# A decode step of cached attention and an MLP on one core: order of the K sums, the pieces of the last K tiles, and the gathers of the output weights

## The chip, the cores and the metric

The kernel runs on one core of a Trainium2 chip. The metric is the device time in microseconds (us) of one execution. Five engines work side by side: TensorE (PE, with its weight loads shown as PEld), VectorE (DVE), ScalarE (ACT), GpSimd (POOL) and SyncE (SP), which here only issues DMAs. The transfers themselves are carried out by 16 DMA engines.

## What is computed

Two tokens (a batch of 2, one position each) pass through a layer norm, an attention over a cache of 8192 positions with 32 heads of width 128, the output projection, a residual, and a pre-norm MLP with another residual. All arrays are float32.

```python
def _A_ref(x, k_cache, v_cache, wq, wo):             # x (2,1,512), caches (2,32,8192,128)
    q = (x @ wq).reshape(B, Sq, H, Dh).transpose(0, 2, 1, 3)
    scores = jnp.einsum("bhqd,bhkd->bhqk", q, k_cache) * (Dh ** -0.5)
    p = _softmax(scores, axis=-1)
    o = jnp.einsum("bhqk,bhkd->bhqd", p, v_cache)
    return o.transpose(0, 2, 1, 3).reshape(B, Sq, H * Dh) @ wo      # wo (4096, 512)

def _B_ref(x, w1, b1, w2, b2):
    y = _layernorm(x)
    return _gelu(y @ w1 + b1) @ w2 + b2              # w1 (512,1792), w2 (1792,512)

h = x + _A_ref(_layernorm(x), k_cache, v_cache, wq, wo)
h2 = h + _B_ref(_layernorm(h), w1, b1, w2, b2)
```

## The kernel before

**Tiles.** The caches are read once, in 32 steps of the main loop (`for i in range(NI)`, line 360). Step i takes one of the two tokens (i modulo 2) and one pair of heads (i divided by 2). Its K tile is 8 MB: 128 partitions, 64 for each of the two heads, each with 128 positions of 128 numbers (64 KB). Its V tile has the same shape. K and V tiles share a ring of three buffers (`BUFS = 3`), so a load waits until the tile three places before it in the ring has been used up. The order of loads is v of step i, then k of step i + 1; near the end k of step 31 comes ahead of v of step 30, and v of step 31 is followed by the weights of the MLP, which take the next buffer of the ring. All of these are issued by SP on one queue. `load` (line 65) takes a list of pieces along the positions; `parts_of` (line 355) says into how many pieces the K tiles 29, 30 and 31 are cut (2, 4 and 2), and V of step 31 comes in four pieces of 64, 32, 24 and 8 positions.

**Scores.** For one query row a matrix product would use little of TensorE, so the scores are made on VectorE. A K tile is worked in four chunks c of 32 positions. `multiply` (line 236) multiplies a chunk by the query; `halve` (line 240) has POOL add the upper half of the 128 products to the lower half; `sums` (line 246) adds up what is left on VectorE. For the first three chunks POOL halves all 32 positions, for the last one 12 of them (`NPOOL`); the other 20 are summed at full width. So in step i and chunk c VectorE is given: the product of chunk c, the sum of the halved part of chunk c - 1, and the sum of the part of chunk c that was not halved. Here they are in the program without a rule for their order; a scheduler places them:

```python
            halve(i, c)
            if i > 0 and c == 0 and not late:
                gather(done)
            if c > 0:
                sums(i, c - 1, True)
            sums(i, c, False)
```

**Softmax and V.** `row_max` (line 250) takes the maximum of each partition on VectorE and transposes the result on TensorE (line 253); `all_max` (line 257) takes the maximum over partitions; a small product (line 260) brings it back to all partitions. `exps` (lines 266 and 271) makes the exponentials on ScalarE. `values` (line 294) multiplies them by the V tile on TensorE in 32 blocks; the profile counts two passes for each. All this is done for step i - 1 while the scores of step i are made. `behind(m)` gives instructions a place in the order of issue after the instruction m.

**The last step.** V of step 30 is multiplied inside step 31, as far as block `MOST` = 24, ahead of the transposed maximum of step 31 (lines 422 to 424). The remaining blocks are put behind that step's `all_max` (line 450). Behind them come the blocks of V of step 31 (lines 506 and 512), and then the projection, the layer norm and the MLP (lines 520 to 573), with a few products in between that only keep TensorE busy (line 478).

**The output weights.** The 4096 rows of `wo` are used as heads are finished. The last 256 rows belong to the last pair of heads and have a load of their own (line 384). The other 3840 rows come in groups (`PLAN`, line 29). An entry 4 is a group of 512 rows, 4 rows of 2 KB for each of 128 partitions, loaded by SP. A tuple is a group in which blocks of four partitions, named by their first partition, get no rows; it has 4 rows for each of the others and is loaded by an indirect DMA that POOL issues (line 135), after POOL has cleared the tile (line 134). The indices of that DMA are built once on VectorE (lines 109 to 117): from the first partition of a left-out block on they are raised by 4096, beyond the bound, which leaves these out, and behind the block they are lowered again, by four more than that. There is one buffer for these groups. A group is used when the heads of its last row are finished: `head_out` (line 329) writes the head rows in the group's layout, `turn` (line 337) transposes them, `turned` (lines 344 and 346) adds their product to `rowacc`. In the step after that the next group is loaded (line 386).

The order of instructions on each engine is fixed when the program is built; each engine works through its own list.

Of the kernel before, what the change touches and what calls it, by code (L numbers as in the profile page):

```python
# [21 lines left out]
BUFS = 3  # L22
NG = 4
WARM = 4
MOST = 24
WR = 4


PLAN = [4, 4,
        (4, 12, 20, 24, 36), 4,  # L30
        (4, 36, 68, 72, 76), 4,
        (4, 36, 112, 116, 120, 124), 4]
FAR = 4096


# [1 line left out]
def tile_decode_block(ctx: ExitStack, tc: tile.TileContext, x, k, v, wq, wo, w1, b1, w2, b2, out):  # L37
# [11 lines left out]
    NI = NM * B  # L49
# [15 lines left out]
    def load(src, i, parts):  # L65
        m, b = divmod(i, B)
        t = kv.tile([P, NS, DH], F32, name="kv", tag="kv")
        rows = src[b, QG * m:QG * m + QG].rearrange("h (p j) d -> (h p) j d", j=NS)
        for s0, n in parts:
            nc.sync.dma_start(t[:, s0:s0 + n], rows[:, s0:s0 + n])  # L70
        return t
# [35 lines left out]
    for _, _, _, blocks in groups:  # L107
        if blocks and blocks not in index:
            acc = work.tile([P, 1], F32, name="ixf")
            nc.vector.tensor_copy(acc, part)  # L110
            for s0 in blocks:
                for edge, step in ((s0, FAR), (s0 + 4, -FAR - 4)):
                    one = work.tile([P, 1], F32, name="ix1")
                    nc.vector.tensor_scalar(one, part, edge - 0.5, float(step), op0=ALU.is_ge, op1=ALU.mult)
                    nc.vector.tensor_add(acc, acc, one)
            index[blocks] = const.tile([P, 1], I32, name=f"ix{len(index)}")
            nc.vector.tensor_copy(index[blocks], acc)
# [7 lines left out]
    def load_wo(g, gate=None):  # L125
        r0, n, r, shut = groups[g]
        t = wts.tile([P, WR, D], F32, name="wog")
        wo_g[g] = t
        if not shut:
            nc.sync.dma_start(t[:, :r], wo[r0:r0 + n, :].rearrange("(p r) n -> p r n", r=r))  # L130
            return
        if gate is not None:
            next_of_pool(lambda: nc.gpsimd.tensor_copy(gate0, gate))
        next_of_pool(lambda: nc.gpsimd.memset(t, 0.0))
        next_of_pool(lambda: nc.gpsimd.indirect_dma_start(
            t.rearrange("p r n -> p (r n)"), None, wo_runs, bass.IndirectOffsetOnAxis(index[shut], 0),
            element_offset=r0 * D, bounds_check=n // r - 1, oob_is_err=False))
# [93 lines left out]
    def multiply(i, c):  # L231
        if c == 0:
            ST[i] = work.tile([P, NS], F32, name="s", bufs=3)
        qb = qps[i // B][:, i % B, None, :].to_broadcast([P, CH, DH])
        kc = kt[i][:, c * CH:(c + 1) * CH, :]
        return nc.vector.tensor_tensor(kc, kc, qb, op=ALU.mult)  # L236
# [5 lines left out]
    def sums(i, c, halved):  # L242
        edge = (c + 1) * CH - NPOOL[c]
        a, e, d = (edge, (c + 1) * CH, DH // 2) if halved else (c * CH, edge, DH)
        if a < e:
            nc.vector.tensor_reduce(ST[i][:, a:e], kt[i][:, a:e, :d], axis=AX.X, op=ALU.add)  # L246
# [8 lines left out]
    def all_max(i):  # L255
        gm = work.tile([1, QG], F32, name="gm")
        last = nc.vector.tensor_reduce(gm, MT.pop(i).rearrange("o (e p) -> o e p", e=QG), axis=AX.X, op=ALU.max,  # L257
                                       negate=True)
        GM[i] = psm.tile([P, QG], F32, name="sm")
        nc.tensor.matmul(GM[i], ones[:1, :], gm, start=True, stop=True)  # L260
        return last

    def exps(i):
        m, b = divmod(i, B)
        nb = work.tile([P, QG], F32, name="nb")
        nc.scalar.activation(nb, GM.pop(i), AF.Copy, scale=SCALE)  # L266
        LT[m] = lt2[:, m % 2]
        s = ST.pop(i).rearrange("p (u j) -> p u j", j=4)
        for e in range(QG):
            ps = slice(e * HP, (e + 1) * HP)  # L270
            nc.scalar.activation(ptz[i % 2][ps, :, 4 * e:4 * e + 4], s[ps], AF.Exp, bias=nb[ps, e:e + 1], scale=SCALE,  # L271
                                 accum_out=LT[m][ps, 32 * e + b:32 * e + b + 1])
# [10 lines left out]
    def inverse(i):  # L283
        if i in RL:
            rl = work.tile(list(RL[i].shape), F32, name="rl" if i >= NI - B else "rlr")
            last = nc.vector.reciprocal(rl, RL[i])
            RL[i] = rl
            return last

    def values(i, us=range(NS // 4)):  # L290
        so = so2[i % 2]
        for u in us:
            n = u % NG
            m = nc.tensor.matmul(so[32 * n:32 * n + 4 * QG], ptz[i % 2][:, u, :], vt[i][:, 4 * u:4 * u + 4, :],  # L294
                                 start=(u < NG), stop=(u >= NS // 4 - NG))
        return m
# [44 lines left out]
    def turned(g):  # L341
        n = groups[g][2]
        t = work.tile([P, WR, B], F32, name="ot4")
        nc.vector.tensor_copy(t[:, :n], TP.pop(g)[:, :n])  # L344
        for r in range(n):
            nc.tensor.matmul(rowacc, t[:, r, :], wo_g[g][:, r, :], start=False,  # L346
                             stop=(g == len(groups) - 1 and r == n - 1))

    def behind(m):
        return tc.issue_after(m.ins)  # L350

    def cut(n):
        return [(j * NS // n, NS // n) for j in range(n)]

    parts_of = {NI - 3: cut(2), NI - 2: cut(4), NI - 1: cut(2)}
    kt, vt = {}, {}
    next_load = 0
    free_from = 1
# [1 line left out]
    for i in range(NI):  # L360
        m, b = divmod(i, B)
        done = i - 1
        late = i == NI - 1
        if not late:
            if i < NI - 2:
                vt[i] = load(v, i, cut(1))
        else:
            vt[i] = load(v, i, [(0, 64), (64, 32), (96, 24), (120, 8)])
            b1r = rows2[:, 0].rearrange("p r q -> p (r q)")[:, :FN]
            nc.vector.memset(b1r, 0.0)  # L370
            b2s = rows2[:B, 1].rearrange("b r q -> b (r q)")
            for e in range(B):
                nc.sync.dma_start(b1r[WB * e::32], b1.rearrange("(n f) -> n f", n=NG))
            nc.sync.dma_start(b2s, b2[None, :].to_broadcast([B, D]))
        if i > 0:
            last = all_max(done)
            exps(done)
            if not late:
                values(done)
        if i < NI - 1:  # L380
            kt[i + 1] = load(k, i + 1, parts_of.get(i + 1, cut(1)))
        if i == NI - 2:
            vt[i] = load(v, i, cut(1))
            nc.sync.dma_start(wl, wo[HL * DH:, :].rearrange("(h p) n -> p h n", p=P))
        if next_load < len(groups) and i == free_from:
            load_wo(next_load, MX[i - 1][:1, 0:1] if next_load == 0 else None)
            next_load += 1
            free_from = NI
        for c in range(NC):
            if i > 0 and c == 0:  # L390
                with behind(last):
                    mul = multiply(i, c)
            else:
                mul = multiply(i, c)
            ended = [g for g in group_end.get(done // B, ())] if done >= 0 and done % B == B - 1 else []
            with behind(mul):
                if i > 0 and c == 1:
                    inverse(done)
                if i > 0 and c == 2 and done % B == B - 1:
                    for h in range(done // B * QG, done // B * QG + QG):  # L400
                        head_out(h)
                if c == 3:
                    for g in ended:
                        turned(g)
                        free_from = i + 1
            halve(i, c)
            if i > 0 and c == 0 and not late:
                gather(done)
            if c > 0:
                sums(i, c - 1, True)  # L410
            sums(i, c, False)
            if i > 0 and c == 0:
                total(done)
            if i > 0 and c == 1 and not late:
                head_sum(done)
            if c == 2:
                for g in ended:
                    turn(g)
        sums(i, NC - 1, True)
        if b == B - 1 and m % 2 == 1 and m + 1 < NM:  # L420
            make_q(m + 1)
        if late:
            with behind(values(done, range(MOST))):
                row_max(i)
        else:
            row_max(i)
# [22 lines left out]
    with behind(last):  # L449
        last = values(hl - 1, range(MOST, NS // 4))  # L450
    gather(hl - 1)
# [148 lines left out]
```

## Time and profile before

| | us |
|---|---|
| median of 3 runs | 1309.41 |
| lowest and highest | 1308.73, 1310.24 |
| the profiled execution, whole | 1309.04 |
| its span, first to last instruction | 1307.3 |

| engine | busy us | share of the span |
|---|---|---|
| VectorE | 941.0 | 72% |
| POOL | 501.7 | 38% |
| TensorE, products | 431.9 | 33% |
| TensorE, weight loads | 128.3 | 10% |
| ScalarE | 63.9 | 5% |

The DMAs move 561.48 MB, on average 430 GB/s over the span. The granted clock of TensorE is 0.652 of full speed on average.

In the lists below, a line of the timeline gives the start and the busy time in us, the engine, the line of the program, the operation, the tile written and the tiles read, the shapes, the number of instructions merged, and in brackets the idle time before it with what ended it. A line of the chain of waits gives the start, the length and what the time was spent on; the chain is followed back from the last instruction. A line of the table by stretches gives the stretch, its length, the busy time and the number of instructions for PE, PEld, DVE, ACT and POOL, then the granted clock of TensorE, the busy share of the DMA engines, and GB/s.

### The profile page before, as it was taken

The numbers are of one execution on the slowest core, as the hardware profiler recorded it, in microseconds if no ns is written. First come the engines' busy times: TensorE is split into PE (matmuls) and PEld (weight loads), VectorE is DVE, ScalarE is ACT, GpSimd is POOL, SyncE is SP. The second block draws the span as 40 slices with busy tenths as digits, with TensorE's granted clock in tenths as the row PEclk, the third lists the DMA queues.
The fourth block names the chain that finished last, engine by engine and source line by source line (L and its number), as shares of the span: only waits on it lengthen the run. The fifth ranks groups of instructions, "written<-read, shape, count | busy, mean of one in ns | idle before, by whom it ended". The sixth has DMA issues, their size and how long they took to land.

```text
span 1307.3 us, 7121 instructions
## 1 busy us (share of the span) xinstructions
PE 431.9 (33%) x2893; PEld 128.3 (10%) x2893; DVE 941.0 (72%) x539; ACT 63.9 (5%) x203; POOL 501.7 (38%) x146
## 2 busy tenths in 40 slices
PE   3033214232331334412344303343213434212528
PEld 0001001010110101100011000101001011000103
DVE  3666688766688676688667697676687767698892
ACT  0000000000000000000000000000000000000001
POOL 0433244432354433344333344333344422444440
PEclk9566656766566666756667556666556666556679
DMA  9999999999999999999999999999999999999997
GB/s 417 429 436 434 431 445 422 442 425 442 429 436 430 438 427 438 428 438 433 434 436 436 432 433 433 434 438 429 440 427 438 433 430 436 423 435 429 441 421 305
DMA packets 12869, 561.48 MB, mean 430 GB/s; under 512 B 1488, under 2 KB 1504, under 8 KB 2148
## 3 DMA queue, kind: packets, MB, share of 16 engines
q1 hardware_dynamic: 12400, 558.39, 98.8%
q0 software_dynamic: 432, 2.62, 0.5%
q8 instruction: 23, 0.38, 0.1%
q14 instruction: 10, 0.08, 0.0%
q10 hardware_dynamic: 4, 0.00, 0.0%
HBM read 561.53 MB, written 0.00 MB: 430 GB/s over the span
## 4 chain that ended last, share of the span: by engine, by line
DMA 37%; DVE 24%; issue 16%; PE 14%; POOL 7%; ACT 1%; POOLq 0%; SPq 0%; DVEq 0%
DMA kv<-in_A_k_cache_dram 37%; DVE kv L236 14%; PE so L294 11%; DVE s L246 9%; POOL kv L240 7%; PE rowacc L346 1%; ACT pt L271 1%; DVE orow L329 1%; PE sm L260 1%; PE sm L253 0%; DVE gm L257 0%; DVE mx L250 0%; PE po L569 0%; PE so L543 0%; ACT nb L266 0%
## 5 line engine op out<-in xcount | busy, mean ns | idle before, releaser
L240 POOL TENSOR_TENSOR kv<-kv 128x2048 f32<-128x2048 f32 (+1 forms) x128 | 490.4, 3844 | 754.1 <-DVE kv L236 540.8
L236 DVE TENSOR_TENSOR kv<-kv,qps 128x4096 f32<-128x4096 f32 x128 | 562.4, 4415 | 301.7 <-DMA kv<-in_A_k_cache_dram 301.5
L246 DVE TENSOR_REDUCE s<-kv 128x32 f32<-128x2048 f32 (+2 forms) x160 | 333.9, 2120 | 21.4 <-POOL kv L240 21.1
L294 PE MATMUL so<-kv,pt 128*8 128x512 f32 x2048 | 282.2, 709 | 55.1 <-ACT pt L271 36.0
L253 PE MATMUL sm<-ident,mx 128*1 128x128 f32 x32 | 11.1, 346 | 495.0 <-DVE mx L250 495.0
L294 PEld LDWEIGHTS so<-kv,pt 128*8 128x8 f32 x2048 | 56.4, 100 | 250.3 <-issue 195.3
L346 PE MATMUL rowacc<-wog,ot 128*2 128x512 f32 x64 | 47.4, 910 | 51.8 <-DVE ot L344 32.3
L221 PE MATMUL qps<-q,pick 2*64 2x256 f32 x64 | 13.8, 577 | 128.8 <-DVE kv L236 128.8
L253 PEld LDWEIGHTS sm<-ident,mx 128*1 128x1 f32 x32 | 2.5, 79 | 519.3 <-issue 283.4
L266 ACT ACTIVATE nb<-sm 128x2 f32<-128x2 f32 x32 | 5.5, 172 | 919.5 <-PE sm L260 919.5
L337 PE MATMUL sm<-ident,orow 2*128 2x2 f32 x32 | 4.6, 244 | 104.3 <-DVE orow L329 104.3
L300 ACT ACTIVATE ss<-so 128x512 f32<-128x512 f32 x31 | 18.5, 597 | 269.4 <-PE so L294 269.4
L314 PE MATMUL sm<-ss,selr 128*34 128x128 f32 x240 | 29.8, 278 | 0.7 <-ACT ss L300 0.7
L314 PEld LDWEIGHTS sm<-ss,selr 128*34 128x34 f32 x240 | 25.6, 115 | 1.8 <-ACT ss L300 1.7
L271 ACT ACTIVATE pt<-s,nb 64x128 f32<-64x128 f32 x64 | 25.5, 399 | 1.4
L260 PE MATMUL sm<-gm,ones 1*128 1x2 f32 x64 | 17.0, 333 | 11.5 <-DVE gm L257 11.5
L257 DVE TENSOR_REDUCE gm<-sm 1x2 f32<-1x128 f32 x32 | 8.9, 279 | 16.4 <-PE sm L253 16.4
L221 PEld LDWEIGHTS qps<-q,pick 2*64 2x64 f32 x64 | 5.5, 192 | 138.1 <-DVE kv L236 134.4
L260 PEld LDWEIGHTS sm<-gm,ones 1*128 1x128 f32 x64 | 14.2, 275 | 21.9 <-DVE gm L257 20.2
L346 PEld LDWEIGHTS rowacc<-wog,ot 128*2 128x2 f32 x64 | 6.6, 111 | 84.8 <-issue 52.1
L337 PEld LDWEIGHTS sm<-ident,orow 2*128 2x128 f32 x32 | 4.0, 209 | 106.4 <-DVE orow L329 63.5
L329 DVE TENSOR_SCALAR orow<-sm,rlr 2x128 f32<-2x128 f32 (+6 forms) x43 | 14.0, 355 | 0.2
(104 smaller groups left out, 115.9 us busy)
## 6 DMA issues: line engine op xcount, KB each, us to landing
kv<-in_A_k_cache_dram SPq DMA_DIRECT2D x4, 4096.0 KB
kv<-in_A_k_cache_dram SPq DMA_DIRECT2D x4, 2048.0 KB, 30.7
ws<-in_B_w_dram SPq DMA_DIRECT2D x3, 1792.0 KB, 16.7
wog<-in_A_wo_dram SPq DMA_DIRECT2D x5, 1024.0 KB, 38.1
kv<-in_A_v_cache_dram SPq DMA_DIRECT2D x1, 4096.0 KB, 30.5
kv<-in_A_v_cache_dram SPq DMA_DIRECT2D x1, 2048.0 KB, 34.9
kv<-in_A_v_cache_dram SPq DMA_DIRECT2D x1, 1536.0 KB, 38.1
ws<-in_B_w_dram SPq DMA_DIRECT2D x1, 1024.0 KB, 16.5
```

The source lines that it names most:

```text
L221: nc.tensor.matmul(t[e * HP:(e + 1) * HP, :, b], pick[32 * n:32 * n + B, b, :], rows[:, :, e], start=True, stop=True)
L236: return nc.vector.tensor_tensor(kc, kc, qb, op=ALU.mult)
L240: return nc.gpsimd.tensor_tensor(t[:, :, :DH // 2], t[:, :, :DH // 2], t[:, :, DH // 2:], op=ALU.add)
L246: nc.vector.tensor_reduce(ST[i][:, a:e], kt[i][:, a:e, :d], axis=AX.X, op=ALU.add)
L253: nc.tensor.transpose(MT[i], mx, ident)
L260: nc.tensor.matmul(GM[i], ones[:1, :], gm, start=True, stop=True)
L271: nc.scalar.activation(ptz[i % 2][ps, :, 4 * e:4 * e + 4], s[ps], AF.Exp, bias=nb[ps, e:e + 1], scale=SCALE, accum_out=LT[m][ps, 32 * e + ...
L294: m = nc.tensor.matmul(so[32 * n:32 * n + 4 * QG], ptz[i % 2][:, u, :], vt[i][:, 4 * u:4 * u + 4, :], start=(u < NG), stop=(u >= NS // 4 - ...
L300: return nc.scalar.activation(SS[i], so2[i % 2], AF.Copy)
L314: nc.tensor.matmul(OP[m], sel_row[:, j, B - 1 - c:B - 1 - c + QR], SS[i - 1 + c][:, j * DH:(j + 1) * DH], start=(c == 0 and j == 0), stop= ...
L329: nc.vector.tensor_scalar(orow[g % 2][:B, :r, p0:p0 + run].rearrange("b r p -> b p r"), OP[h // QG][r0e:r0e + B, c0:c0 + run * r].rearrang ...
L346: nc.tensor.matmul(rowacc, t[:, r, :], wo_g[g][:, r, :], start=False, stop=(g == len(groups) - 1 and r == n - 1))
```

## The change

Five things differ.

1. The sums of a step and chunk are given a place in the order of issue behind the product of the same chunk.
2. K tile 29 is loaded in one piece instead of two, tile 30 in two instead of four; tile 31 stays at two.
3. The 3840 rows come in nine groups instead of eight: four with left-out blocks instead of three (384 rows each instead of 432, 432 and 416), four of 512 rows instead of five, and one of 256 rows. The left-out blocks are 32 instead of 16, and other ones. The last group is now one with left-out blocks; it is loaded in step 29 and used in step 30.
4. Where two left-out blocks touch, the table of indices is built without the edge between them.
5. `MOST` is 8 instead of 24.

```diff
-MOST = 24
+MOST = 8

 PLAN = [4, 4,
-        (4, 12, 20, 24, 36), 4,
-        (4, 36, 68, 72, 76), 4,
-        (4, 36, 112, 116, 120, 124), 4]
+        (0, 4, 68, 72, 76, 80, 84, 88), 4,
+        (36, 48, 100, 104, 108, 112, 116, 120), 4,
+        (4, 12, 20, 24, 68, 72, 76, 80), 2,
+        (12, 20, 24, 44, 52, 56, 116, 120)]
...
             nc.vector.tensor_copy(acc, part)
-            for s0 in blocks:
-                for edge, step in ((s0, FAR), (s0 + 4, -FAR - 4)):
+            ends = [p for s0 in blocks for p in (s0, s0 + 4)]
+            for p in sorted(set(ends)):
+                if ends.count(p) == 1:
+                    if p in blocks:
+                        edge, step, first = p, FAR, p
+                    else:
+                        edge, step = p, first - p - FAR
                     one = work.tile([P, 1], F32, name="ix1")
                     nc.vector.tensor_scalar(one, part, edge - 0.5, float(step), op0=ALU.is_ge, op1=ALU.mult)
                     nc.vector.tensor_add(acc, acc, one)
...
-    parts_of = {NI - 3: cut(2), NI - 2: cut(4), NI - 1: cut(2)}
+    parts_of = {NI - 2: cut(2), NI - 1: cut(2)}
...
-            if c > 0:
-                sums(i, c - 1, True)
-            sums(i, c, False)
+            with behind(mul):
+                if c > 0:
+                    sums(i, c - 1, True)
+                sums(i, c, False)
```

## The prediction

> **What bounds the kernel now.** I read the utilisation page first, then the records of the DMA packets, then the chain of waits and the timelines of VectorE and TensorE over the last 130 us.
>
> ```profile
> PE 431.9 (33%) x2893; PEld 128.3 (10%) x2893; DVE 941.0 (72%) x539; ACT 63.9 (5%) x203; POOL 501.7 (38%) x146
> DMA  9999999999999999999999999999999999999997
> q1 hardware_dynamic: 12400, 558.39, 98.8%
> ```
>
> The DMA row is at nine tenths in every slice but the last and the loads' queue alone fills 98.8% of the 16 engines' span, while VectorE has 28% to spare. The packet records say more. A packet starts 3 to 4 ns before another ends, so the records can be strung into 16 streams. None is idle between the first packet and 1293.8 us (but for two gaps of 0.2 us in one), and a 64 KB packet takes 2.418 us in every stream. So up to there only bytes count, and they stay the same (561 MB). What can change is which stream is last, and what the engines do behind the last K tiles:
>
> ```profile
> 1175.42 8.75 DVE L236 TENSOR_TENSOR kv<-kv,qps 128x4096 f32<-128x4096 f32 x2 [1.13 <-DMA kv<-in_A_k_cache_dram]
> 1189.15 2.29 DVE L246 TENSOR_REDUCE s<-kv 128x32 f32<-128x2048 f32 x1 [2.18 <-POOL kv L240]
> ...
> 1209.35 4.42 DVE L236 TENSOR_TENSOR kv<-kv,qps 128x4096 f32<-128x4096 f32 x1 [1.93 <-DMA kv<-in_A_k_cache_dram]
> 1218.59 2.29 DVE L246 TENSOR_REDUCE s<-kv 128x32 f32<-128x2048 f32 x1 [4.82 <-POOL kv L240]
> ...
> 1243.89 8.73 DVE L236 TENSOR_TENSOR kv<-kv,qps 128x4096 f32<-128x4096 f32 x2
> ...
> 1257.44 2.29 DVE L246 TENSOR_REDUCE s<-kv 128x32 f32<-128x2048 f32 x1 [2.17 <-POOL kv L240]
> 1259.65 8.74 DVE L236 TENSOR_TENSOR kv<-kv,qps 128x4096 f32<-128x4096 f32 x2
> 1268.74 5.87 DVE L246 TENSOR_REDUCE s<-kv 128x32 f32<-128x2048 f32 x3 [0.35 <-POOL kv L240]
> 1274.65 0.29 DVE L250 TENSOR_REDUCE mx<-s 128x1 f32<-128x128 f32 x1
> ```
>
> Tile 30 starts at 1209.35 when its first quarter lands (1208.90). From there VectorE is the bound: it waits 4.82 and 2.17 us for GpSimd's halving, and is never again short of K. Behind it TensorE sets the end:
>
> ```profile
> 1275.08 0.37 PE sm L253
> 1275.45 1.81 PE so L294 x2
> 1277.26 0.51 PE sm L260 x2
> 1277.77 2.48 PE so L294 x14
> 1280.26 0.31 PE sm L278 x2
> 1280.57 3.55 PE so L294 x32
> ```
>
> This chain runs on without a gap to the output product at 1300.64; the last packet of w2 landed at 1300.04, and its four products come last in 3.3 us. So the final landing has about 3 us to spare; K's landings and TensorE's queue behind the transpose at 1275.08 (call it T) do not.
>
> **Part 1: order and pieces of the last K tiles.** In the built program only tiles 29, 30 and 31 change order; all others already alternate product, sum, product, sum. Their price is two undisturbed tiles of this trace: tile 27, from its first product (1105.24) to the end of its L257 maximum, 29.2 us; tile 26, the same with a clearing of the bias row, two head rows and a copy, 30.4 us (1066.57 to 1096.95).
>
> When do they start? Tile 29 is now one load. Before, its halves landed at 1175.04 and 1184.72, the latter in the latest stream. By then the changed kernel has moved 3456 rows of wo instead of 3840, and the late streams have rows left out (part 2). Stream by stream I get 1182.4 for the latest. With the 0.5 us from landing to product seen at 1208.90 and 1209.35, tile 29 starts at 1182.9 instead of 1175.4 and ends at 1212.1. VectorE stands idle for these 7 us, which by itself costs nothing: the first half of tile 30 lands at 1212.5 (before 1213.77 for the same bytes), so tile 30 starts at 1213.0. It is tile 26 with four head rows (0.225, 0.41, 0.41, 0.225) instead of two (0.86): 30.8 us, to 1243.8. Its second half (1222.2) is there before its third product. Tile 31, landed at 1241.6, starts at 1243.7; T follows 28.5 us after its first product, as in tile 27: 1272.2. **T comes 2.9 us earlier.** If that cover were gone, each us by which the first half of tile 30 is late would go straight into T.
>
> What hangs on the later end of tile 29: SP may issue the load of tile 31 only when tile 29's buffer is free, now about 1211 instead of 1206. The queue then still holds tile 30 until 1220.3 on the quickest stream, so it costs nothing unless tile 29 ends 8 us later still. The load of v29 waits for tile 28 (1173.3); the quickest stream is dry at 1179.5, before 1177.2. The SP loads queued behind these have more room.
>
> **Part 2: the gathers.** A partition left out shows as a 4 B packet of 9 ns instead of an 8 KB one of 309. In the three gathers, rows 4 and 36 always vanish from the same stream, so I take p and p+32 to share one. A stream moves 64 - 4c packets of 8 KB for wo now and 68 - 4c after, with c its blocks left out; packets follow each other at 0.305 us.
>
> ```
> rows of the stream             c now  after   us      last packet ends now -> after
> 12|20|24, 68|72|76             1      3      -1.2     1297.8..1300.03 -> 1296.6..1298.8
> 112|116|120                    1      3      -1.2     1299.4..1300.00 -> 1298.2..1298.8
> 4 (and 36)                     6      3      +4.9     1293.8 -> 1298.7
> 124                            1      0      +2.4     1296.0 -> 1298.4
> five never left out            0      0 or 1  +1.2 or 0   1296.6..1298.1 -> 1296.6..1299.3
> ```
>
> The spread of 6 us becomes about 2, the end 1.2 us earlier (at worst 0.7): for K this is in the landings above, for w2 it is worth nothing. The fourth gather adds 20 ns of empty packets per stream. On POOL it adds a clearing (1.80) and an issue (1.16) between tiles 28 and 29, where POOL idles for 10.7 us (until 1180.07). The clearing waits for the products of the group before, with tile 29's halving queued behind it; that needs tile 29's first product, now at 1187. It lands 27 us after issue, near 1200, and is used at 1236. The shorter table of edges is built under the first loads (first K tile at 42.6 us).
>
> **Part 3: MOST 24 to 8.** Not in the title, and it costs. v30 lands at 1262.17; TensorE then does 24 of its 32 blocks in 6.72 us, done at 1269.3, long before T. Now 8 go there and 24 come behind T, in front of the last V tile. From T the rows above give 0.30 to the first block, 1.81 for it, 0.51 for L260, 2.5 for eight blocks (now seven), 0.31 for L278: T + 5.4 both ways. Then 15 more blocks of two passes: 32 passes take 3.55, so 30 take 3.35. **The last V tile starts at T + 8.8 instead of T + 5.4.** The exponentials that it needs end at T + 3.9 and do not bind; its pieces (up to 1281.6) and w1 (1285.9, 1290.1) have landed in time. Nothing after 1280.5 has a gap that takes this up.
>
> ```profile
> 1275.00:1278.00 3.00, 2.92 (x9) 0.80 (x13) 2.17 (x5) 0.17 (x1) 0.00 (x0) 0.50 0.98 409
> 1278.00:1284.00 6.00, 6.00 (x48) 1.33 (x40) 2.34 (x5) 2.95 (x7) 0.00 (x0) 0.91 1.02 433
> ```
>
> The clock column (0.50, 0.91) bounds this price. The clock opens at 1279.07, 3.7 us after TensorE resumes; at half clock four passes take 0.85 instead of 0.43. If it opens right after T, half of the 2.5 us is saved in both kernels; if 3.4 us later, the changed kernel loses 1.3. I keep 3.35, from 2.5 to 4.7.
>
> [...]
>
> **Sum.** -2.9 (T) + 3.35 (blocks behind T) = +0.45 us. Against the profiled execution (span 1307.3, 1.7 around it, 1309.04) that is 1309.5; the median of the runs (1309.41) lies 0.37 above it, so 1309.9. The K side is good to 1 us (landings and four estimated head rows), TensorE's from -0.9 to +1.3.
>
> **Rivals.** (a) *TensorE's remainder is covered.* If the last V tile were held by something else until about 1280.5, or the blocks ran beside the exponentials at full clock, the 2.9 us of T would be kept: 1306.5, faster. For it: TensorE would otherwise stand idle from T + 0.4 to T + 3.9. Against: the 9 blocks now there already run past T + 3.9.
>
> (b) *The left-out rows miss the late streams.* The places of 80, 84, 88 and of 112 to 124 rest on one pair seen (4 and 36), and of the four streams of 112 to 124 three end at 1299.4 to 1300.0 and one at 1296.0. If 124 is a late one, it ends at 1302.4, tile 30's first half lands near 1216.1 instead of 1212.5, and T with it: +0.45 + 3.6, 1313.5, slower. It decides from 2.2 us of extra lateness on. Against: program fetches (16 KB, each 1.4 us with the stall behind it) go round eight streams in a fixed order and pass two of 68 to 76, then three of 112 to 124 in one run, so the one passed over is most simply the last, 124.
>
> [...]
>
> (c) *One load for tile 29 costs more than it frees.* Tile 29 has 0.9 us to spare before tile 30 may start; beyond that each us goes into T. Landed at 1186 instead of 1182.4 it would give +0.45 + 2.7, 1312.6, slower; it decides from 3.1 us late. Against: the latest stream would have to be 1.3 us behind today's 1184.72 with 384 rows of wo fewer moved. That the forced order does not hold is no rival: the built program has it.
>
> **Chances.** A difference under 0.2% (2.6 us) is about what a measurement of this kernel can tell from none. My sum, with its bounds, lies within it: 0.56. Rival (a) and a better K side: 0.23, faster by over 0.2%, of which (a) alone is just beyond the bound (1306.8). (b) 0.10, (c) and a late clock with a smaller gain 0.11: slower 0.21. The likeliest time is 1309.9, its own range 1308.0 to 1311.8; to hold 8 in 10 it reaches to (a) and half way to (b): 1306.2 to 1312.6.
>
> **What will show it.** Right, if: tile 29's first product starts near 1183 and tile 30's near 1213, both released by DMA; no sum of tiles 29 to 31 waits 2 us for POOL; T near 1272; behind T 15 blocks after L278, and the last V tile's first block near 1281; last w2 packet near 1299. Wrong, if tile 30 starts after 1215, if any stream runs dry between 1180 and 1240, or if the last V tile starts under 7 us after T.

## The result and the profile after

| | before | after |
|---|---|---|
| median of 6 runs each, same chip | 1309.49 us | 1314.79 us |
| lowest and highest | 1308.73, 1310.30 | 1313.55, 1315.66 |
| the profiled execution, and its span | 1309.04, 1307.3 | 1314.36, 1312.6 |

The changed kernel is slower: the ratio is 1.0039 (95% interval 1.0026 to 1.0052), 5.3 us by the medians. The forecast was 1309.9 with a range that ended at 1312.6; the time lies above it.

The page of after, utilisation and the queue of the loads:

```profile
PE 436.6 (33%) x2899; PEld 128.7 (10%) x2899; DVE 939.7 (72%) x533; ACT 64.1 (5%) x203; POOL 505.1 (38%) x149
DMA  9999999999999999999999999999999999999996
q1 hardware_dynamic: 11968, 557.87, 98.5%
```

The DMAs are still busy throughout and move half a megabyte less on this queue (the gathers' queue moves it instead, 3.15 MB against 2.62). Nothing here shows a loss. The timeline of VectorE around the last three K tiles does:

```profile
1186.04 8.75 DVE L242 TENSOR_TENSOR kv<-kv,qps 128x4096 f32<-128x4096 f32 x2 [9.54 <-DMA kv<-in_A_k_cache_dram]
...
1216.40 8.75 DVE L242 TENSOR_TENSOR kv<-kv,qps 128x4096 f32<-128x4096 f32 x2 [1.23 <-DMA kv<-in_A_k_cache_dram]
1226.26 0.16 DVE L292 RECIPROCAL rlr<-sm 34x1 f32<-34x1 f32 x1 [1.11 <-PE sm L287]
...
1247.69 8.73 DVE L242 TENSOR_TENSOR kv<-kv,qps 128x4096 f32<-128x4096 f32 x2
...
1275.74 0.29 DVE L256 TENSOR_REDUCE mx<-s 128x1 f32<-128x128 f32 x1
```

Tile 29 starts at 1186.04, tile 30 at 1216.40, both held by DMA as foreseen, and both over 3 us later than foreseen. The 2 us waits for POOL in tiles 29 to 31 are gone: tile 31 takes 28.05 us from its first product to its maximum (30.76 before). In tile 30 there is a wait that was not foreseen, 1.11 us of a reciprocal for TensorE. T is 1276.17 instead of 1272.2. The chain of waits from there, and TensorE's clock in the table by stretches:

```profile
1276.17 0.37 PE sm L259
1276.54 1.81 PE so L300 x2
1278.35 0.51 PE sm L266 x2
1278.86 3.53 PE so L300 x16
1282.39 0.36 PE sm L284 x2
1282.75 6.98 PE so L300 x62
```

```profile
1276.00:1278.00 2.00, 1.83 (x3) 0.18 (x3) 1.41 (x4) 0.00 (x0) 0.00 (x0) 0.50 1.01 430
1278.00:1282.00 4.00, 4.00 (x19) 0.94 (x18) 0.78 (x3) 2.64 (x7) 0.00 (x0) 0.50 0.99 417
1282.00:1290.00 8.00, 8.00 (x71) 2.33 (x68) 2.34 (x5) 0.60 (x1) 0.00 (x0) 0.97 1.02 425
```

The 62 passes are the 30 left of v30 and the 32 first ones of the last V tile, so that tile starts near 1282.75 + 3.35 = 1286.1, T + 9.9. The clock stays at 0.50 up to 1282; the 16 passes ahead of L284 take 3.53 us where 14 took 2.48 before. From the last V tile on everything is a copy of before, 5.6 us later.

Why did the loads land late? The records of the packets tell. The table holds all kernels that bear on this, those of the experiments below too; "step" is the mean time between the starts of two 64 KB packets that follow each other in one stream, from 400 to 1150 us.

```
                  K, V buffers   median packet, ns       step, ns
                  start at       8 KB  16 KB  64 KB      64 KB
before            24064          309   611    2418       2414.2
after             24096          313   614    2421       2419.2
a_aligned         24064          309   611    2418       2414.1
b_shift32         24096          313   614    2421       2419.1
b_shift64         24128          312   613    2420       2418.2
b_shift128        24192          311   614    2420       2417.9
b_shift256        24320          309   611    2418       2414.1
```

After, a packet of 8, 16 or 64 KB takes 3 to 4 ns more by its median, and the step between 64 KB packets is 5 ns longer, in all 16 streams alike (2419.2 to 2419.3 ns in each). The 496 packets of 64 KB of a stream make some 2.5 us of it, the smaller ones 0.6 more by their medians. The first column is what the program gives: every tile has a place in the on-chip memory at a byte address within each partition. The fourth group of gathers has a fourth tile of indices, 32 bytes. It stands ahead of the K and V buffers and moves them by 32 bytes.

### The profile page after: what moved, and what is told of

Read it like the earlier page. It is cut to its first block, busy times and chain, and to the rows that moved or that the text cites. A ratio compares the mean times of both kernels' runs of the same rounds, so it can differ in the third digit from the quotient of the medians.

```text
span 1312.6 us, 7132 instructions
## 1 busy us (share of the span) xinstructions
PE 436.6 (33%) x2899; PEld 128.7 (10%) x2899; DVE 939.7 (72%) x533; ACT 64.1 (5%) x203; POOL 505.1 (38%) x149
## 3 DMA queue, kind: packets, MB, share of 16 engines
q0 software_dynamic: 576, 3.15, 0.6%
## 4 chain that ended last, share of the span: by engine, by line
DMA 44%; DVE 32%; PE 14%; POOL 6%; issue 2%; ACT 1%; another core or an unknown queue 1%; POOLq 0%; SPq 0%; DVEq 0%
DMA kv<-in_A_k_cache_dram 44%; DVE kv L242 17%; DVE s L252 14%; PE so L300 11%; POOL kv L246 6%; ACT pt L277 1%; PE sm L266 1%; PE sm L259 0%; DVE mx L256 0%; DVE gm L263 0%; PE po L576 0%; PE so L550 0%; ACT nb L272 0%; PE sm L314 0%
## 5 line engine op out<-in xcount | busy, mean ns | idle before, releaser
L300 PE MATMUL so<-kv,pt 128*8 128x512 f32 x2048 | 285.5, 716 | 55.0 <-ACT pt L277 37.3
```

## The experiments

In the names, b_ is the kernel before with one or two edits, a_ the kernel after with some of them taken back.

**The address and MOST, each alone and both: a_most24, a_aligned, a_aligned_most24, b_shift32.**

```diff
 # a_most24
-MOST = 8
+MOST = 24
 # a_aligned: 32 bytes fewer ahead of the buffers
-    epst = const.tile([P, 1], F32, name="epst")
-    eps2 = const.tile([P, 1], F32, name="eps2")
+    epss = const.tile([P, 2], F32, name="epss")
+    epst, eps2 = epss[:, 0:1], epss[:, 1:2]
 # b_shift32: 32 bytes more ahead of the buffers
+    const.tile([P, 8], F32, name="shift")
     part = const.tile([P, 1], F32, name="part")
```

> The kernel after with MOST = 24 again, nothing else. Theory: the change lost in two separate places, up to 4 us in loads that land late and some 4.5 us in TensorE's remainder behind T, of which the third edit is the second. So: loads as late as after (tile 31's K near 1245.0, T near 1276.2), last V tile starts near T + 5.4 instead of T + 9.9, time 1310 to 1311.5, that is 3.3 to 4.5 us under the kernel after. Rival: the remainder is hidden behind the loads' lateness, and the time stays within 1 us of the kernel after.

> The kernel after with the two EPS constants in one tile of 32 bytes, so that the fourth index tile no longer moves what lies behind it: the K and V buffers stand at 24064, 89600 and 155136 bytes again, as in the kernel before, instead of 32 bytes higher. Theory (address): the 32 bytes made every large packet slower; steps between 64 KB packets 2414 ns as before instead of 2419, tile 31's K lands near 1242, T at 1272.2 to 1273.5, time 1311 to 1312, some 3 us under the kernel after. Rival (plan): the gathers' other rows bring the streams into step with each other; nothing changes, 2419 ns, 1314.8. Rival (chance of a run): 2419 in some runs and 2414 in others, with the address either way.

> Both of these: MOST = 24 and the buffers at the addresses of the kernel before. Theory (address): step 2414 ns, T 1272.2 to 1273.5, last V tile starts at T + 5.4, time 1306.5 to 1308, faster than before by 1.5 to 3 us. Rival (plan): as the kernel after with MOST = 24 alone, 1310 to 1311.5.

> The kernel before with an unused constant tile of 32 bytes ahead of the others, so that the K and V buffers stand 32 bytes higher, as in the kernel after; nothing else. Theory (address): steps of 2419 ns between 64 KB packets instead of 2414, loads of the last tiles some 2.5 to 3 us late, time 1312 to 1312.7. Rivals (plan, chance): 1309.4, as before.

| kernel | median us | before, same chip | ratio, 95% interval |
|---|---|---|---|
| a_most24 | 1311.56 | 1309.82 | 1.0012, 1.0003 to 1.0021 |
| a_aligned | 1311.64 | 1309.82 | 1.0016, 1.0007 to 1.0025 |
| a_aligned_most24 | 1308.08 | 1309.82 | 0.9986, 0.9977 to 0.9995 |
| b_shift32 | 1312.94 | 1309.82 | 1.0023, 1.0014 to 1.0033 |

The address is the cause of the late loads. Undone in the kernel after, it brings the packets back to 2414 ns and the time down by 3.5 us (5.3 over its own before for after, 1.8 for a_aligned); put into the kernel before, with nothing else, it costs 3.1. The plan of the gathers and the chance of a run are out: all three profiles with the buffers at 24096 (after, a_most24, b_shift32) have the slow packets, and none of those at 24064 has them. What is shown is the address. All that lies behind the added tile moves with the K and V buffers, and how the place slows a packet is not shown. MOST is worth 3.6 us (5.3 against 1.7), and the same again with the address put right (1.8 against -1.7): the two add up. Two details were missed. The last V tile of a_most24 starts at T + 6.4 instead of T + 5.4, since the clock opens late there too. And with the address put right T is 1274.00 (a_aligned) and 1273.79 (a_aligned_most24), later than the 1272.2 to 1273.5 that were expected.

The timeline of VectorE in a_aligned shows what is left:

```profile
1182.88 8.75 DVE L242 TENSOR_TENSOR kv<-kv,qps 128x4096 f32<-128x4096 f32 x2 [9.38 <-DMA kv<-in_A_k_cache_dram]
...
1213.46 8.75 DVE L242 TENSOR_TENSOR kv<-kv,qps 128x4096 f32<-128x4096 f32 x2 [1.43 <-DMA kv<-in_A_k_cache_dram]
1224.08 0.16 DVE L292 RECIPROCAL rlr<-sm 34x1 f32<-34x1 f32 x1 [1.87 <-PE sm L287]
...
1245.52 8.73 DVE L242 TENSOR_TENSOR kv<-kv,qps 128x4096 f32<-128x4096 f32 x2
```

Tile 29 starts at 1182.88 where the prediction has 1182.9, tile 30 at 1213.46 (1213.0). Tile 30 takes 32.06 us to the next tile's start instead of 30.8, with 1.87 us spent waiting at the reciprocal. TensorE's timeline of a_aligned shows what it waits for, the product L287 behind the 64 passes of the values of tile 29:

```profile
1213.95 9.94 PE L300 MATMUL so<-kv,pt 128*8 128x512 f32 x64 [1.29 <-ACT pt L277]
1223.82 0.23 PE L287 MATMUL sm<-ones,ls 128*34 128x1 f32 x2
```

**Which multiple counts: b_shift64, b_shift128, b_shift256.** The same edit as b_shift32 with 64, 128 and 256 bytes; for 128 and 256 six small tiles of the start have one buffer instead of two, to make room.

> The kernel before with an unused constant tile of 64 bytes instead of the 32 of the earlier run: the K and V buffers at 24128, 89664 and 155200 bytes. If a multiple of 64 bytes is enough for the packets: steps of 2414 ns between them and 1309.4 to 1310, as before. If they need a multiple of 128 or more: steps of 2416 to 2419 ns and 1311 to 1313.

> The kernel before with 128 bytes of unused constants (and one buffer instead of two for six small tiles of the start, to make room): K and V buffers at 24192, 89728 and 155264 bytes, multiples of 128 and not of 256. If a multiple of 128 is enough: a 64 KB packet takes 2418 ns, an 8 KB one 309, and 1309.4 to 1310. If it takes a multiple of 256: 2420 ns, 312, and 1311 to 1313, as with 64 bytes.

> The same with 256 bytes: buffers at 24320, 89856 and 155392 bytes, multiples of 256 and not of 512. If a multiple of 256 is enough: 2418 ns, 309, and 1309.4 to 1310. If it takes a multiple of 512: 2420 ns, 312, and 1311 to 1313.

Measured: 64 bytes 1312.46 us (ratio 1.0019, 1.0009 to 1.0028), 128 bytes 1312.19 (1.0019, 1.0009 to 1.0028), 256 bytes 1309.43 (1.0000, 0.9990 to 1.0009). The packets say the same (table above). So of the places tried the two on a multiple of 256 bytes are the quick ones, and a multiple of 64 or 128 is not enough. b_shift256 has the same six single buffers as b_shift128, so these are not the cause. From 8 KB to 64 KB the price does not grow with the size of the packet (4 ns for 8 KB, a step longer by 5 for 64 KB). By what mechanism the place costs it the runs do not show, and two things speak against one fixed price for each packet. The price is not there at the start of the execution (last section). And it is not one price: between 400 and 1150 us 99% of the 64 KB packets of before took 2418 ns, while of those of after 54% took 2421 and 21% took 2428.

**Order and pieces apart: b_order, b_pieces, b_order_pieces.** Each is the kernel before with the hunk named, from the diff of the change: the sums placed `behind(mul)`, the new `parts_of`, and both. MOST and the gathers are those of before, and so are the addresses.

> The kernel before with the first edit alone: the sums forced in order between K's products; pieces, gathers and MOST as before. Theory: the order takes two waits of 2.2 us for GpSimd out of tile 31, which then runs 28.0 us from its first product to its maximum instead of 30.8; T falls from 1275.1 to some 1272.5, and the time to 1306.5 to 1307.5 (about -2.5). Rival (the reciprocal): in tile 30 the reciprocal on VectorE now comes before TensorE has finished the values of tile 29 and waits; where that wait is over 1.5 us and K of tile 31 is already there, the gain is half of it or less: 1308 to 1309.

> The kernel before with the pieces alone: K of tile 29 in one load, of tile 30 in two; the order left to the planner. Theory: tile 29 can't start before the whole of it has landed (some 1184.3 instead of 1175.4), so that its 28 to 31 us end 7 us later than before, at 1213 to 1215, just when tile 30's first half is there; tile 30 then runs without its 4.8 us wait. T within 1.5 us of before either way, time 1308 to 1311. Rival (one load costs more than it frees): 3 us late and more, 1312 to 1313.

> The kernel before with order and pieces both, and the gathers and MOST of before: three index tiles, so that the buffers stand where they stood. It differs from the kernel after with both fixes only in the gathers. Theory: the new gathers bring K's landing about 1 us forward; so this one is about 1 us slower than that one, T near 1274.4, 1308.5 to 1309.5. Rival: the gathers bring nothing at T, and it takes 1307.5 to 1308.3, the same as the kernel after with both fixes. Rival: the old gathers' spread of 7.5 us over the streams holds back a load that now matters, and it takes 1310 and more.

| kernel | median us | before, same chip | ratio, 95% interval |
|---|---|---|---|
| b_order | 1306.31 | 1310.01 | 0.9974, 0.9964 to 0.9984 |
| b_pieces | 1309.21 | 1310.01 | 0.9996, 0.9987 to 1.0006 |
| b_order_pieces | 1309.32 | 1310.01 | 0.9995, 0.9986 to 1.0005 |

The order alone wins 3.7 us, more than either theory allowed; with the pieces beside it 3 us of that are gone. The expectation priced tile 31 alone, and with two waits of 2.2 us where the rows of before have one, of 2.17. The order also takes the 4.82 us wait for GpSimd out of tile 30: tile 31 starts at 1239.63 instead of 1243.89. The timelines of VectorE, first b_order, then b_order_pieces:

```profile
1175.41 8.75 DVE L236 TENSOR_TENSOR kv<-kv,qps 128x4096 f32<-128x4096 f32 x2 [1.13 <-DMA kv<-in_A_k_cache_dram]
...
1209.29 4.42 DVE L236 TENSOR_TENSOR kv<-kv,qps 128x4096 f32<-128x4096 f32 x1 [4.54 <-DMA kv<-in_A_k_cache_dram]
1214.09 4.42 DVE L236 TENSOR_TENSOR kv<-kv,qps 128x4096 f32<-128x4096 f32 x1 [0.37 <-DMA kv<-in_A_k_cache_dram]
1218.42 0.15 DVE L286 RECIPROCAL rlr<-sm 34x1 f32<-34x1 f32 x1
...
1239.63 8.73 DVE L236 TENSOR_TENSOR kv<-kv,qps 128x4096 f32<-128x4096 f32 x2
...
1267.68 0.29 DVE L250 TENSOR_REDUCE mx<-s 128x1 f32<-128x128 f32 x1
1269.69 0.28 DVE L257 TENSOR_REDUCE gm<-sm 1x2 f32<-1x128 f32 x1 [1.73 <-PE sm L253]
```

```profile
1185.25 8.75 DVE L236 TENSOR_TENSOR kv<-kv,qps 128x4096 f32<-128x4096 f32 x2 [11.03 <-DMA kv<-in_A_k_cache_dram]
...
1214.45 8.73 DVE L236 TENSOR_TENSOR kv<-kv,qps 128x4096 f32<-128x4096 f32 x2
1226.65 0.16 DVE L286 RECIPROCAL rlr<-sm 34x1 f32<-34x1 f32 x1 [3.46 <-PE sm L281]
...
1247.67 8.73 DVE L236 TENSOR_TENSOR kv<-kv,qps 128x4096 f32<-128x4096 f32 x2
...
1275.72 0.28 DVE L250 TENSOR_REDUCE mx<-s 128x1 f32<-128x128 f32 x1
```

With the old pieces tile 30 starts on its first quarter at 1209.29 and works its second at 1214.09, when that lands; the product that the reciprocal needs (L281) ran on TensorE at 1206.67, ahead of the values of tile 29, so it waits for nothing. The maximum of tile 31 is there at 1267.68, 8 us earlier than with the new pieces. With those, tile 29 waits 11 us for all of its K, tile 30 starts 5.2 us later, and the reciprocal waits 3.46 us for L281, which now stands on TensorE behind the 64 passes of the values of tile 29 (10.01 us from 1216.45 on). b_pieces has this too (2.62 us), but its tile 31 already runs in 28.04 us: with other landings the scheduler (the planner of the expectations) chose the good order by itself. The two edits are therefore two ways to the same 2.7 us, and the one brings a new wait. Beside the pieces the order adds nothing that these runs can tell (-0.80 us for b_pieces, -0.69 for b_order_pieces). T of b_order_pieces was expected near 1274.4 and is 1276.15; its time lies in the range expected.

Against before, the maximum of b_order is 7 us earlier (1267.68 instead of 1274.65). Why that becomes 3.7 in the time is in TensorE's timeline of b_order, and in its chain of waits:

```profile
1262.59 6.86 PE L294 MATMUL so<-kv,pt 128*8 128x512 f32 x48 [20.78 <-DMA kv<-in_A_v_cache_dram]
1269.38 0.27 PE L253 MATMUL sm<-ident,mx 128*1 128x128 f32 x1
...
1273.57 3.62 PE L294 MATMUL so<-kv,pt 128*8 128x512 f32 x32 [0.52 <-DMA kv<-in_A_v_cache_dram]
...
1291.96 1.33 PE L544 MATMUL so<-ws,ones 128*32 128x448 f32 x12 [1.59 <-DMA ws<-in_B_w_dram]
```

```profile
1239.92 43.52 DMA kv<-in_A_v_cache_dram
1283.45 0.02 issue
1283.46 16.36 DMA ws<-in_B_w_dram
1299.82 0.04 issue
1299.87 1.10 PE po L570 x24
```

The maximum now waits for v30's passes, and behind it waits for loads of V and w1 have appeared (0.52 and 1.59 us). The chain from 1239.92 to 1299.82 is loads alone: they are the bound again.

**The reciprocal and the gathers: a_best_inv, a_best_parts.** Both start from a_aligned_most24.

```diff
 # a_best_inv
-                if i > 0 and c == 1:
+                if i > 0 and c == (2 if i == NI - 2 else 1):
                     inverse(done)
 # a_best_parts
-    parts_of = {NI - 2: cut(2), NI - 1: cut(2)}
+    parts_of = {NI - 3: cut(2), NI - 2: cut(4), NI - 1: cut(2)}
```

> The kernel after with MOST = 24, the buffers at the old addresses, and the reciprocal of tile 29's sums put a chunk later (in tile 30's third chunk instead of its second). Theory: VectorE's wait of 1.45 us for TensorE in tile 30 goes, T falls from 1273.8 to 1272.3 or 1272.4, the time by 1.2 to 1.5 us, to 1306.5 to 1307. Rival: the last loads of w2 (landing at 1299.6) then set the end, and at most 0.5 us of it is seen.

> The kernel after with MOST = 24, the buffers at the old addresses, and K of tiles 29 and 30 in two and four loads as before: of the change, the order and the gathers are left. Theory: the pieces undid what the order had won; with them back tile 29 starts near 1174, the maximum of tile 31 comes near 1267 on VectorE and the loads set the end; the gathers then bring them about 0.7 us forward and at a spread of 3.3 us instead of 7.2, so it is 0.5 to 1.2 us faster than the kernel before with the order alone (1306.3): 1305.1 to 1305.8. Rival: the gathers bring nothing beside the order, 1306.3.

a_best_inv takes 1307.01 us (before 1310.01, ratio 0.9974, 0.9963 to 0.9985), 1.3 better than a_aligned_most24, each against its own before; the two intervals overlap, so by the times alone this is not clear of noise. In its profile the wait is gone, tile 30 takes 30.5 us instead of 31.6, and T is 1272.55 instead of 1273.79:

```profile
1213.59 8.75 DVE L242 TENSOR_TENSOR kv<-kv,qps 128x4096 f32<-128x4096 f32 x2 [1.45 <-DMA kv<-in_A_k_cache_dram]
...
1229.29 0.15 DVE L292 RECIPROCAL rlr<-sm 34x1 f32<-34x1 f32 x1
...
1244.08 8.73 DVE L242 TENSOR_TENSOR kv<-kv,qps 128x4096 f32<-128x4096 f32 x2
```

But the execution shown gains nothing in time (1307.42 against 1307.16 us). TensorE's passes ahead of L284, first a_aligned_most24, then a_best_inv:

```profile
1276.41 2.28 PE L300 MATMUL so<-kv,pt 128*8 128x512 f32 x14
1278.62 0.38 PE L284 MATMUL sm<-ls,ones 128*128 128x2 f32 x2
```

```profile
1275.17 3.60 PE L300 MATMUL so<-kv,pt 128*8 128x512 f32 x14
1278.70 0.57 PE L284 MATMUL sm<-ls,ones 128*128 128x2 f32 x2
```

The same 14 passes take 3.60 us at half clock, and L284 comes at the same time: the granted clock opens at 1277.22 in the one and at 1279.10 in the other. In these two executions the 1.24 us that T is earlier went into the later opening of the clock; the eight runs of this kernel range over 2.8 us.

a_best_parts takes 1305.41 us (before 1309.92, ratio 0.9967, 0.9955 to 0.9979): 4.5 us faster than before and the lowest median of all. The 0.8 us that it is ahead of b_order lie within the two intervals. It is the change without the pieces, without MOST = 8 and without the 32 bytes. Its end, in TensorE's timeline, waits for each piece of w2:

```profile
1295.76 1.74 PE L576 MATMUL po<-ws,pt 128*32 128x128 f32 x56 [0.31 <-DMA ws<-in_B_w_dram]
1298.11 1.08 PE L576 MATMUL po<-ws,pt 128*32 128x128 f32 x32 [0.62 <-DMA ws<-in_B_w_dram]
1299.36 1.04 PE L576 MATMUL po<-ws,pt 128*32 128x128 f32 x24 [0.17 <-DMA ws<-in_B_w_dram]
```

From before to after, one edit at a time. T is that of the one profiled execution of each kernel, the medians are of all its runs, so the two columns need not move together. (The profiled execution of b_order_pieces is the slowest of its ten.) The interval of b_order lies clear of 1, and for the pieces, MOST and the 32 bytes the intervals of the two ratios do not overlap; for the gathers they do.

| kernel | edit added | T | median minus its before, us | step |
|---|---|---|---|---|
| before | | 1275.08 | 0 | |
| b_order | order | 1269.38 | -3.70 | -3.7 |
| b_order_pieces | pieces | 1276.15 | -0.69 | +3.0 |
| a_aligned_most24 | gathers | 1273.79 | -1.74 | -1.1 |
| a_aligned | MOST 8 | 1274.00 | +1.82 | +3.6 |
| after | 32 bytes | 1276.17 | +5.30 | +3.5 |

## Why the prediction was wrong

**"So up to there only bytes count, and they stay the same."** This is the step that failed. The bytes stayed the same, their price did not: 2419 ns a packet instead of 2414, some 3 us at the last K tiles and 3.5 us in the time (a_aligned against after; 3.1 in b_shift32). The forecast was +0.45 us and +5.30 came: these 3.5 are most of what is missing. I had taken 2.418 us as a property of the streams, and it was one of the place where the tiles lay. The diff shows a fourth index tile; where the buffers stand in the built program would have shown the 32 bytes, though not their price, which no row of before has.

**"It is tile 26 with four head rows [...]: 30.8 us, to 1243.8."** The second failure, 1.3 us in a_aligned. Tile 30 starts 2.6 us after the maximum of tile 29, and TensorE, at half clock until 1219.8, then has 9.9 us of that tile's values ahead of the product that the reciprocal on VectorE waits for. The reciprocal stands behind the second product of tile 30 and ahead of its sums, and holds them up; I costed the products, sums and head rows and not this wait. With the reciprocal a chunk later the tile takes 30.5 us (a_best_inv), as priced.

**"T comes 2.9 us earlier."** Without the address it came 1.1 to 1.3 us earlier: the 2.9, less 0.5 for the start of tile 30 and 1.3 for its length. With it T was 1.1 us later than before. Between a_aligned and after T moved by 2.2 us and the span by 3.4; in these two executions the rest is the clock, which opened 6.3 us after T instead of 3.8. The starts of tile 29 and 30 were right to 0.5 us (a_aligned), and tile 31 took the 28.5 us to T that were priced. But order and pieces were priced as one sum, and so the best part of the answer was missed: of the two, the order is worth 3.7 us alone and the pieces take 3.0 back. "VectorE stands idle for these 7 us, which by itself costs nothing" held only against a tile 30 that can't start before its half; the old quarters had let it start 4 to 5 us earlier.

**The gathers.** 1.2 us forward foreseen. Kernels that differ in them alone are 1.1 us apart with the new pieces (a_aligned_most24 and b_order_pieces; tile 29 starts 2.1 us earlier) and 0.8 us with the old ones (a_best_parts and b_order, each against its own before). Neither is clear of noise by the times alone, as the intervals overlap both times; the earlier landing is seen in one profile of each. No loss is seen, and no late stream.

**MOST.** +3.35 foreseen, 3.6 measured, twice. The clock was the bound named for it: in the profile after it opened 6.0 us after TensorE resumed instead of 3.7, which put the last V tile at T + 9.9 instead of T + 8.8. In a_aligned_most24 the delay, counted the same way, was 3.1 us. The range up to 4.7 supposed an opening 3.4 us later than before; no run here shows one, and the latest opening seen, in a_best_inv, is 2.6 later (6.6 us after T instead of 4.0).

**The rivals.** (a) did not happen: nothing covered the remainder, a_most24 and a_aligned_most24 show its full price. (b) gave a time near the measured one, by a mechanism that was absent: no stream is late, all 16 lose alike. That its 1313.5 lies nearest to what came is luck. (c), a K tile 29 that lands over 3.1 us late, is what the profile shows (1185.5 instead of 1182.4), but not for its reason: with the address put right the same load landed in time. Nor did it act as described: in after tile 30 is held by its own load (1.23 us for DMA), not by tile 29. With the old gathers it did act, as in b_order_pieces tile 30 starts right behind tile 29. A rival on the price of a packet was missing.

## What to carry to other kernels

Where the loads fill the time, check the byte address of their buffers in the built program whenever a small tile is added or taken away ahead of them: here multiples of 256 bytes were the quick ones, 256 bytes of padding cost nothing measurable (1309.43 us), and the place was worth 3 us of 1310. Price each part of a change alone as well as in the sum: two edits that remove the same wait do not add up, and one of them may bring a wait of its own. When an instruction is pinned to an earlier place in an engine's order, everything that stands ahead of it there, a reciprocal of the tile before for instance, is to be checked for what it waits for.

## What the hardware showed that I had not expected

- In these kernels, loads into buffers that do not start on a multiple of 256 bytes (24096, 24128, 24192) took 2 to 4 ns more per packet by the medians, on packets of 8 to 64 KB, and the step between 64 KB packets was 4 to 5 ns longer. It does not show at once: in after the steps are 2415.3 ns up to 80 us, the same as in before, 2418.4 from 80 to 120 us (2416.0 in before) and 2419.2 from 180 us on (2414.1 to 2414.8). Why it starts late is open, and with it how the address makes a packet longer.
- In b_order TensorE is busy right up to T, with the 48 passes of v30 (6.86 us), and the granted clock is already 1.00 there (1267 to 1273 us): the 14 passes take 1.90 us instead of 2.3 to 3.6. The six runs of a_best_parts range over 0.5 us, the nine of b_order over 1.2, those of the kernels whose clock opens behind T over 1.5 to 2.8. That the time at which the clock opens makes this spread is not shown, as no run isolates it: in the two steady kernels the loads set the end, and this alone could keep the clock out of the time.
